# Token pairs in the first four chunks, fp32 weights on SyncE's queue and transposes by DMA in a fused linear-attention and cosine-MLP kernel

## The chip, the cores and the metric

The kernel runs on one core of a Trainium2 chip. The metric is the device time of one execution in microseconds; lower is better. Before the change it is 232.49 us, the median of three runs (231.07 to 234.35).

## The reference

Two stages follow each other. The first is a gated linear attention over 4 batches x 8 heads x 768 tokens with head size 48; the second is a two-layer network with the activation h*cos(h) on the 3072 tokens of 384 features that come out of it.

```python
f = 1.0 / (1.0 + np.exp(-f_logit))
for t in range(S):
    state = f[:, :, t, :, None] * state + np.einsum('bhd,bhe->bhde', k[:, :, t], v[:, :, t])
    y[:, :, t] = np.einsum('bhd,bhde->bhe', q[:, :, t], state)
x = y.transpose(0, 2, 1, 3).reshape(B * S, H * D)
h = x @ w_in                      # 384 -> 2048
g = h * np.cos(h)
out = g @ w_out                   # 2048 -> 384
```

All inputs and the output are fp32 in HBM; the products run in bf16 with fp32 accumulation.

## The kernel before, in words

**Chunks.** The tokens are cut into 24 chunks of 128 tokens, six to a batch. The recurrence is done chunk by chunk: within a chunk it is a masked product of queries and keys, and between chunks a state of 48 x 48 per head is carried. Chunks 0, 6, 12 and 18 start a batch and have no state to take in; chunks 5, 11, 17 and 23 end one and pass none on.

**Loads.** Each chunk needs f_logit, k, q and v, 192 KB each (L329), 128 tokens on 128 partitions and the 8 heads side by side. One token of one head is 48 fp32 numbers, so each of these transfers consists of 1024 pieces of 192 bytes. All of them stand on SyncE's queue (SP) except q and v of chunk 0, which ScalarE issues. The weights, 3 MB each for w_in and w_out, are loaded in four pieces each by GpSimd (L320), whose queue converts them to bf16 on the way. Each SP transfer waits for the transfer eight places earlier to land.

**Decay.** For a group of one or two chunks ScalarE computes exp (L345) and ln (L353) of the forget gate, TensorE sums over tokens with a triangular mask (L361, L364, called cum below), and ScalarE takes two exponentials of the sums (L371, called eb and ei). These four use one table of ScalarE functions and the cosine of the second stage another, so groups are collected (GROUPS): the exps of a collected group wait for all its f loads, and each change of table costs a load of it (L567, L496).

**Attention of a chunk n.** GpSimd, in the first chunks also VectorE, multiplies q and k with the decays (qk, L384) and casts v (vb, L388). TensorE transposes the 8 blocks of 128x128 of qk (tr, L398), ScalarE or VectorE copies them from PSUM to SBUF (qkt, L402). TensorE makes the scores (sc, L414), VectorE masks them (am, L417). TensorE makes the state's increment (ps, L428), VectorE adds it (st, L437), GpSimd scales it (sz, L443). TensorE makes the output (y, L453 and L457), a copy casts it (yb), TensorE transposes its 3 blocks (trx, L470) and a copy brings them into xT (xe, both copies L402).

**The network.** It runs over units of tokens: unit 0 is chunk 0, unit 1 chunk 1, and units 2 to 12 are two chunks each. A unit of 256 tokens has eight pieces h (L489, 6 matmuls each; two pieces fill one of two PSUM places of two banks), four cosines (L496), four products g (L499), and for each of its two chunks four pieces o (L509, 4 matmuls each), a copy ot (L512) and a store (L516). Units 0 and 1 have four pieces h of 12 narrower matmuls, two cosines and four pieces o. Piece h number j reads the w_in piece j (units 0 and 1) or j // 2 (the others); piece o number s of a chunk reads w_out piece s.

**Order.** A planner in the program (Plan.run) places all operations on the engines by their costs and priorities, and the kernel records them in that order; on the chip each engine works through its own list and waits by semaphores. Priorities before are a chunk's or unit's number plus a constant (LEAD_H, LEAD_O).

Of the kernel before, what the change touches and what calls it, by code (L numbers as in the profile page):

```python
# [15 lines left out]
class Slots:  # L16


    def __init__(self, aps, name):
        self.aps, self.name = aps, name  # L20
        self.free_at = [0.0] * len(aps)
        self.held = [False] * len(aps)

# [17 lines left out]
class Banks:  # L41
# [20 lines left out]
    def used(self, s, t):  # L62
        for i in range(s, s + self.size):
            self.base["free"][i] = max(self.base["free"][i], t)

# [35 lines left out]
class Op:  # L101
    __slots__ = ("seq", "eng", "fn", "prio", "table", "deps", "vals", "alloc", "start", "end",
                 "lat", "waiting", "after", "grp", "dma", "name", "late")


class Plan:
# [37 lines left out]
    def run(self):  # L144
        free = dict.fromkeys(("PE", "ACT", "DVE", "POOL", "SP"), 0.0)
        table, lock, bus = None, None, {}
# [9 lines left out]
        while len(order) < n:  # L156
            cand = []
            for o in ready:
                at, pe = o.late, "PE" in o.eng
# [39 lines left out]
            for v in o.alloc:  # L199
                if v.slot is None:  # L200
                    v.slot = v.pool.best()[1]
                    v.pool.take(v.slot)
            o.start = s
            free[e] = s + cost
            if o.dma is not None:
                kb, rate = o.dma
                ring = "POOL" if e == "POOL" else "SP"
                bus[ring] = max(s + cost, bus.get(ring, 0.0)) + kb * 1e3 / rate
                o.end = bus[ring] + 1700.0
# [21 lines left out]
GROUPS = [(1, 1), (2,), (2, 2), (2, 2), (2, 2), (2, 2), (2, 2)]  # L231
UNITS = [128, 128] + [256] * 11
LEAD_H, LEAD_O = 2.31, 9.45
ANCHOR = [None, None, 2, 10, 18, 26, 34]


def build(nc, cpool, ppool, q, k, v, f_logit, moe_w_in, moe_w_out, out):
# [29 lines left out]
    def zpad(t):  # L267
# [10 lines left out]
    vbS = slots("vb", 4, [128, HD])  # L278
    qktS = slots("qkt", 3, [128, 2 * NP, C])
# [4 lines left out]
    x_sb = [tl([128, KM, 256], BF16, f"xT_{i}") for i in range(n_tokens // 256)]  # L284
    gS = slots("gT", 4, [128, KF, 256])
# [5 lines left out]
    base = {"held": [False] * 8, "free": [0.0] * 8,  # L291
            "tiles": [ppool.tile([128, 1024], F32, name=f"ps_{i}") for i in range(4)]}
    phS = Banks(base, 2, [0, 2], "ph")
    scS = Banks(base, 2, [4, 6], "sc")
    p1S = Banks(base, 1, [7, 6, 5, 4], "p1")
# [18 lines left out]
    def load_weights(part, i, prio, late):  # L314
        def fn(e):
# [4 lines left out]
            nc.gpsimd.dma_start(out=dst.ap, in_=src)  # L320
        dst = w_in_v[i] if part == 0 else w_out_v[i]
        P.op(f"w{part}{i}", {"POOL": 900.0}, fn, writes=[dst], prio=prio, dma=(786, 230), late=late)

    def issue(e):
        return {"SP": nc.sync, "ACT": nc.scalar, "POOL": nc.gpsimd}[e]

    def load(t, src, b, c, prio, eng, nm):
        def fn(e):
            issue(e).dma_start(out=t.ap, in_=src[b, :, c * C:(c + 1) * C, :].rearrange("h p d -> p h d"))  # L329
        P.op(nm, {eng: 480.0}, fn, writes=[t], prio=prio, dma=(196, 240))  # L330

    xT = [Val(ap=x_sb[n // 2][:, :, n % 2 * C:n % 2 * C + C] if nc is not None else None)
          for n in range(n_tokens // C)]
    state = {}

    def decay(chunks, g, prio):
# [4 lines left out]
        for i, (b, c, n, ld) in enumerate(chunks):  # L341
            load(ft.part(lambda a, i=i: a[:, i]), f_logit, b, c, n - 0.4, "SP", f"f{n}")
# [5 lines left out]
        gates.append((first, ANCHOR[g]))  # L348
# [4 lines left out]
        P.op("ln", {"ACT": act(384 * m, "S")}, lambda e: nc.scalar.activation(  # L353
# [246 lines left out]
```

## Time and profile before

| what | value |
|---|---|
| median of 3 runs | 232.49 us |
| the profiled execution's own time | 231.37 us |
| its span in the trace | 229.5 us |
| TensorE (PE) busy | 184.0 us, 80% |
| PE weight loads (PEld) busy | 136.5 us, 59% |
| VectorE (DVE) busy | 122.4 us, 53% |
| ScalarE (ACT) busy | 134.2 us, 58% |
| GpSimd (POOL) busy | 78.9 us, 34% |
| bytes moved | 27.05 MB in 107030 packets, 100352 of them under 512 bytes |

The profile lists busy times by engine, the span in 40 slices of 5.74 us with a digit for each engine's busy tenths, the DMA queues, the chain of work that ended last (each step followed back to what released it), and groups of instructions by line. A matmul's busy time includes the time it spends in the pipeline, so what a run of matmuls really costs TensorE is read from one start to the next.

### The profile page before, as it was taken

What the parts mean: (1) busy time and instruction counts of PE and PEld (TensorE: products, weight loads), DVE (VectorE), ACT (ScalarE), POOL (GpSimd) and SP (SyncE); (2) the same over time, 40 slices, a digit from 0 to 9 for tenths busy, and PEclk for the clock granted to TensorE, in tenths of its full rate; (3) what the DMA queues carried; (4) which work ended last, traced back from release to release, by engine and by line L of the source; (5) the groups of instructions that cost most, each with busy time, mean ns of one, the idle gap of its engine ahead of it and who ended that gap; (6) DMA issues with size and microseconds to landing.
All of it is one profiled execution on the core that took longest, in us unless ns stands there. A gap on an engine that the chain in (4) does not pass through costs nothing.

```text
span 229.5 us, 4755 instructions
## 1 busy us (share of the span) xinstructions
PE 184.0 (80%) x1936; PEld 136.5 (59%) x1936; DVE 122.4 (53%) x150; ACT 134.2 (58%) x163; POOL 78.9 (34%) x121
## 2 busy tenths in 40 slices
PE   0230498455999987999979999989999899999993
PEld 0120398324777756787658776677775677776551
DVE  1150259303788629794095971568852888665000
ACT  3400667483566885758867667856688675654111
POOL 6401772029602087400763222750208611000000
PEclk9999999955799999999999999999999999999999
DMA  8999999899999398803799224781001010100211
GB/s 132 213 193 196 185 200 191 162 199 188 184 194 176 82 223 164 155 13 93 141 210 199 49 60 103 174 174 32 3 34 39 34 37 0 39 0 34 73 69 69
DMA packets 107030, 27.05 MB, mean 118 GB/s; under 512 B 100352, under 2 KB 107008, under 8 KB 107008
## 3 DMA queue, kind: packets, MB, share of 16 engines
q1 hardware_dynamic: 101216, 23.21, 53.0%
q0 software_dynamic: 3712, 3.15, 8.5%
q10 hardware_dynamic: 2080, 0.39, 1.1%
q8 instruction: 15, 0.25, 0.5%
q14 instruction: 7, 0.06, 0.1%
HBM read 25.17 MB, written 4.72 MB: 130 GB/s over the span
## 4 chain that ended last, share of the span: by engine, by line
PE 56%; DVE 11%; ACT 10%; SPq 9%; DMA 8%; issue 3%; POOL 1%; DVEq 0%; ACTq 0%; POOLq 0%
PE ps L509 25%; PE ps L489 20%; SPq L329 9%; DMA f<-in_f_logit_dram 7%; ACT qkt L402 4%; DVE gT L499 4%; PE ps L414 3%; DVE am L417 2%; PE ps L398 2%; DVE qkt L402 2%; PE ps L470 2%; DMA k<-in_k_dram 2%; ACT f L345 1%; PE ps L361 1%; DVE st L437 1%
## 5 line engine op out<-in xcount | busy, mean ns | idle before, releaser
L509 PE MATMUL ps<-w_out_bf,gT 128*128 128x384 bf16 x384 | 73.1, 330 | 6.0 <-ACT qkt L402 2.0
L489 PE MATMUL ps<-xT,w_in_bf 128*128 128x256 bf16 (+1 forms) x624 | 76.3, 270 | 1.7 <-DVE gT L499 1.7
L496 ACT ACTIVATE cosh<-ps,halfpi 128x1024 bf16<-128x1024 f32 x48 | 53.0, 1115 | 28.1 <-PE ps L489 28.0
L499 DVE TENSOR_TENSOR gT<-ps,cosh 128x1024 bf16<-128x1024 f32 x48 | 58.1, 1219 | 13.2 <-ACT cosh L496 13.0
L489 PEld LDWEIGHTS <-w_in_bf 128*128 128x128 bf16 x624 | 56.7, 101 | 11.2 <-issue 2.1
L509 PEld LDWEIGHTS <-gT 128*128 128x128 bf16 x384 | 36.1, 98 | 26.8 <-issue 8.4
L388 POOL CAST vb<-v 128x384 bf16<-128x384 f32 x24 | 12.5, 519 | 66.6 <-PE ps L457 27.8
L417 DVE TENSOR_TENSOR am<-ps,umask 128x1024 bf16<-128x1024 f32 x24 | 29.3, 1219 | 6.5 <-PE ps L414 6.4
L398 PE MATMUL ps<-ident,qk 128*128 128x128 bf16 x192 | 16.5, 234 | 14.6 <-POOL qk L384 13.2
L384 POOL TENSOR_TENSOR qk<-q,b 128x384 bf16<-128x384 f32 x21 | 21.0, 999 | 20.5 <-ACT b L371 12.9
L443 POOL TENSOR_TENSOR sz<-st,b 64x192 bf16<-64x192 f32 x32 | 16.0, 501 | 23.5 <-DVE st L437 22.2
L398 PEld LDWEIGHTS <-qk 128*128 128x128 bf16 x192 | 13.0, 103 | 17.5 <-POOL qk L384 14.4
L384 POOL TENSOR_TENSOR qk<-k,bi 128x384 bf16<-128x384 f32 x22 | 22.3, 1013 | 0.3
L345 ACT ACTIVATE f<-f 128x768 f32<-128x768 f32 (+1 forms) x13 | 9.9, 789 | 20.3 <-DMA f<-in_f_logit_dram 20.2
L402 ACT COPY qkt<-ps 128x1024 bf16<-128x1024 bf16 x13 | 13.2, 1012 | 10.3 <-PE ps L509 9.1
L361 PE MATMUL ps<-sp,umask 128*128 128x384 bf16 x24 | 8.1, 363 | 13.3 <-ACT sp L353 12.1
L402 DVE COPY qkt<-ps 128x1024 bf16<-128x1024 bf16 x11 | 7.6, 688 | 20.3 <-PE ps L509 10.6
L437 DVE TENSOR_TENSOR st<-ps,sz 128x384 f32<-128x384 f32 x16 | 8.8, 552 | 12.5 <-ACT qkt L402 11.1
L512 DVE COPY ot<-ps 128x384 f32<-128x384 f32 x12 | 6.6, 554 | 16.5 <-PE ps L509 12.0
L371 ACT ACTIVATE b<-ps 128x776 f32<-128x776 f32 (+1 forms) x13 | 10.0, 768 | 8.8 <-PE ps L364 8.5
L414 PE MATMUL ps<-qkt 48*128 48x128 bf16 x192 | 10.2, 229 | 5.6 <-DVE st L437 2.4
L364 PEld LDWEIGHTS <-sp 128*128 128x128 bf16 x96 | 5.7, 101 | 14.9 <-issue 13.5
(37 smaller groups left out, 150.8 us busy)
## 6 DMA issues: line engine op xcount, KB each, us to landing
f<-in_f_logit_dram SPq DMA_DIRECT2D x24, 192.0 KB, 4.6
k<-in_k_dram SPq DMA_DIRECT2D x24, 192.0 KB, 4.4
out_dram<-ot SPq DMA_DIRECT2D x24, 192.0 KB, 1.9
q<-in_q_dram SPq DMA_DIRECT2D x23, 192.0 KB, 4.3
v<-in_v_dram SPq DMA_DIRECT2D x23, 192.0 KB, 4.4
w_in_bf<-in_moe_w_in_dram POOLq DMA_DIRECT2D x4, 384.0 KB, 6.9
w_out_bf<-in_moe_w_out_dram POOLq DMA_DIRECT2D x4, 384.0 KB, 7.9
q<-in_q_dram ACTq DMA_DIRECT2D x1, 192.0 KB, 4.1
```

Of the source, the lines that this page charges most:

```text
L329: issue(e).dma_start(out=t.ap, in_=src[b, :, c * C:(c + 1) * C, :].rearrange("h p d -> p h d"))
L384: lambda e, j=j, src=src, dec=dec: E(e).tensor_mul(out=qk.ap[:, j, :, 0:D], in0=src.ap, in1=HB(dec.ap[:, i, 0:HD])),
L388: P.op("vb", {"POOL": 560.0}, lambda e: nc.gpsimd.tensor_copy(out=vb.ap, in_=vf.ap.rearrange("p h d -> p (h d)")), reads=[vf], writes=[vb] ...
L398: nc.tensor.transpose(out=o[:, j * NP + p, :], in_=pair(j, p), identity=ident)
L402: (nc.scalar.copy if e == "ACT" else nc.vector.tensor_copy)(out=o, in_=i_)
L414: nc.tensor.matmul(o[:, r, p, :], lhsT=qkt.ap[s, NP + p, :], rhs=qkt.ap[s, p, :], start=(p == 0), stop=(p == NP - 1))
L417: P.op("am", {"DVE": dve(1024)}, lambda e: nc.vector.tensor_mul(out=am.ap.rearrange("p r a n -> p (r a) n"), in0=sc.ap.rearrange("p (a n) ...
L443: eng().tensor_mul(out=S_out.ap[s, :, r, :], in0=srcap()[s, :, r, :], in1=bt.ap[s, i, HD:, None].broadcast_to([64, NP, D]))
L489: nc.tensor.matmul(ph.ap[:, g * T:(g + 1) * T], lhsT=w_in_bf[:, m, f0:f0 + 128], rhs=x[:, m, :], start=(g % (G // 2) == 0 and m == 0), sto ...
L496: nc.scalar.activation(out=co.ap, in_=ph.ap, func=AF.Sin, bias=halfpi),
L499: P.op("g", {"DVE": dve(1024)}, lambda e, ph=ph, co=co, gv=gv: nc.vector.tensor_mul(out=gv.ap, in0=ph.ap.rearrange("p (g t) -> p g t", t=T ...
L509: nc.tensor.matmul(po.ap[:, 0:d_model], lhsT=gT.ap[:, j, i * C:(i + 1) * C], rhs=w_out_bf[:, j, :], start=(j == 0), stop=(j == KF - 1))
```

## The change

Five things are changed together.

1. **Pairs.** In chunks 0 to 3 (NPAIR = 4) a partition holds two neighbouring tokens of four heads instead of one token of eight: partitions 0 to 63 take heads 0 to 3, partitions 64 to 127 heads 4 to 7. A piece of a transfer is then 384 bytes and there are 512 of them, in two transfers of 64 partitions each, issued one after the other. cum, tr, sc, ps and y have a form of their own for it, with new masks (incl, strict, pmask, half), a v tile with zeros (vp, filled by two casts) and more or wider matmuls: cum has 3 matmuls for 1 beside 4 narrow ones, sc 16 for 8, ps and y twice the columns. The stores of these chunks are two of 64 partitions.
2. **Weights.** They are loaded as fp32 on SP's queue into places of gT and cast to bf16 by an operation wc on GpSimd, VectorE or ScalarE. gT has 6 places for 4; xT has 5 places that are used again, for 12 that were not.
3. **Transposes by DMA.** In chunks 14 to 22 the 8 blocks of qk go from SBUF to SBUF by one DMA transpose on SP's queue (tq) instead of tr and qkt; in chunks 12 to 22 the 3 blocks of yb do (ty) instead of trx and xe.
4. **PSUM.** h has three places for two, single-bank results six banks for four, both overlapping with others.
5. **Order.** GROUPS is cut otherwise, with single chunks first; the priorities are a table (PR) with an entry for each load, decay, chunk, turn and unit, and the exps of the first collected group no longer wait for all of its f loads. The planner's costs and its model of the DMA queue are changed.

```diff
-GROUPS = [(1, 1), (2,), (2, 2), (2, 2), (2, 2), (2, 2), (2, 2)]
+GROUPS = [(1, 1, 1), (1,), (2,), (2, 2), (2, 2), (2, 2), (2, 2), (2,)]
 UNITS = [128, 128] + [256] * 11
-LEAD_H, LEAD_O = 2.31, 9.45
-ANCHOR = [None, None, 2, 10, 18, 26, 34]
+NPAIR = 4
+FREE_GROUPS = 1
+TURN_QK = range(14, 23)
+TURN_Y = range(12, 23)
+PR = {
...
-    gS = slots("gT", 4, [128, KF, 256])
+    xS = slots("xT", 5, [128, KM, 256])
+    gS = slots("gT", 6, [128, KF, 256])
...
-    phS = Banks(base, 2, [0, 2], "ph")
-    scS = Banks(base, 2, [4, 6], "sc")
-    p1S = Banks(base, 1, [7, 6, 5, 4], "p1")
+    phS = Banks(base, 2, [0, 2, 4], "ph")
+    scS = Banks(base, 2, [4, 6, 2], "sc")
+    p1S = Banks(base, 1, [7, 6, 5, 4, 3, 2], "p1")
...
-            nc.gpsimd.dma_start(out=dst.ap, in_=src)
-        P.op(f"w{part}{i}", {"POOL": 900.0}, fn, writes=[dst], prio=prio, dma=(786, 230), late=late)
+            nc.sync.dma_start(out=view(), in_=src)
+        P.op(f"w{part}{i}", {"SP": 420.0}, fn, writes=[stage], prio=prio, dma=2080.0)
+        P.op("wc", {"POOL": 2100.0, "DVE": 900.0, "ACT": act(1536, "S")}, lambda e:
+             cast(e, dst.ap, view()), reads=[stage], writes=[dst], prio=PR["wc"][4 * part + i])
...
+            for r in range(2):
+                (nc.scalar if e == "ACT" else nc.sync).dma_start(
+                    out=t.ap[64 * r:64 * r + 64].rearrange("p (h e) d -> p h (e d)", e=2),
+                    in_=tok[4 * r:4 * r + 4].rearrange("h (p e) d -> p h (e d)", e=2))
...
-        for o in firsts[g]:
-            o.deps.update(loads)
+        if g >= FREE_GROUPS:
+            for o in firsts[g]:
+                o.deps.update(loads)
...
-        P.op("tr", {"PE": mm(128, 8)}, tr, reads=[qk], writes=[pt], prio=prio)
+        if n in TURN_QK:
+            P.op("tq", {"SP": 420.0}, lambda e: nc.sync.dma_start_transpose(
+                out=qkt.ap, in_=qk.ap.rearrange("p j h d -> p (j h d)")),
+                reads=[qk], writes=[qkt], prio=PR["tq"][n], dma=2000.0)
+        else:
+            pt = Val(p1S)
+            P.op("tr", {"PE": mm(128, 8)}, tr, reads=[qk], writes=[pt], prio=prio)
...
-        px, x = Val(p1S), xT[n]
+        x = xT[n]
+        if n in TURN_Y:
+            P.op("ty", {"SP": 420.0}, lambda e: nc.sync.dma_start_transpose(out=x.ap, in_=yb.ap),
+                 reads=[yb], writes=[x], prio=PR["ty"][n], dma=1200.0)
+            return
```

The first place is the start of SP's list, before the change: f, k, q, v by 192 KB (the number behind a name is the buffer).

```order
L329 DMA f_73<-in_f_logit_dram 128x8x48
L329 DMA k_76<-in_k_dram 128x8x48
L329 DMA f_74<-in_f_logit_dram 128x8x48
L329 DMA k_77<-in_k_dram 128x8x48
L329 DMA q_81<-in_q_dram 128x8x48
L329 DMA v_85<-in_v_dram 128x8x48
L329 DMA f_75<-in_f_logit_dram 128x8x48
L329 DMA k_78<-in_k_dram 128x8x48
```

The same place with the change: L383 are weight pieces into gT, L399 halves of a paired load (x2 is one load), L396 loads of a chunk from 4 on.

```order
L383 DMA gT_160<-in_moe_w_in_dram 128x3x512
L399 DMA f_94<-in_f_logit_dram 64x4x96 x2
L399 DMA v_105<-in_v_dram 64x4x96 x2
L399 DMA v_106<-in_v_dram 64x4x96 x2
L399 DMA f_95<-in_f_logit_dram 64x4x96 x2
L399 DMA f_96<-in_f_logit_dram 64x4x96 x2
L399 DMA k_97<-in_k_dram 64x4x96 x2
L399 DMA k_98<-in_k_dram 64x4x96 x2
L399 DMA q_102<-in_q_dram 64x4x96 x2
L383 DMA gT_161<-in_moe_w_in_dram 128x3x512
L399 DMA v_107<-in_v_dram 64x4x96 x2
L396 DMA k_99<-in_k_dram 128x8x48
```

A weight piece now stands first, the three f of chunks 0 to 2 come before k and q, and a chunk from 4 on already has its k in row 12. Up to and with the last w_in piece, row 24, SP's list has 4 weight pieces, 15 paired loads (q of chunk 0, the sixteenth, is on ScalarE) and 5 whole loads; from row 25 to k of chunk 6, row 39, it has 12 whole loads and the 4 w_out pieces.

The second place is PE's list around the scores of chunk 14, before: tr (L398) of chunk 14, a piece h around the transposes of an output (L470), and sc (L414); one row stands for each group of equal rows and their weight loads.

```order
L398 MATMUL ps_155<-ident,qk_102 128x128
...
L489 MATMUL ps_153<-xT_133,w_in_bf 128x256
...
L470 MATMUL ps_156<-ident,yb_127 128x128
...
L489 MATMUL ps_153<-xT_133,w_in_bf 128x256
...
L414 MATMUL ps_155<-qkt_114 128x128
```

The same place with the change, from ps (L575) of chunk 14 to its scores (L550): L671 are matmuls of o, 8 and 4 of them, L651 of h, 12 and 12, and the second L575 is ps of chunk 15.

```order
L575 MATMUL ps_178<-vb_131,qk_125 128x96
...
L671 MATMUL ps_178<-w_out_bf,gT_161 128x384
...
L651 MATMUL ps_177<-xT_157,w_in_bf 128x256
...
L651 MATMUL ps_175<-xT_157,w_in_bf 128x256
...
L575 MATMUL ps_178<-vb_130,qk_124 128x96
...
L671 MATMUL ps_178<-w_out_bf,gT_161 128x384
...
L550 MATMUL ps_176<-qkt_141 128x128
```

The transposes are gone from this place, and between ps, which needs the same qk as the turn, and the scores, which need the turned one, there is now work of the network.

The third place is SP's list in the second half, with the change: turns of qk (L517) and of yb (L622) among stores (L685) and loads; before, no transposes stood on this list.

```order
L517 DMA_TRANSPOSE qkt_139<-qk_123 128x8x128
L396 DMA k_97<-in_k_dram 128x8x48
L396 DMA q_102<-in_q_dram 128x8x48
L685 DMA out_dram<-ot_169 128x384
L622 DMA_TRANSPOSE xT_158<-yb_154 128x3x128
L517 DMA_TRANSPOSE qkt_141<-qk_125 128x8x128
L396 DMA k_98<-in_k_dram 128x8x48
```

Nine L517 and eleven L622 stand on this list from its row 84 on. A load behind a turn is issued only when the turn's qk or yb has been written.

## Rows read from the trace of the kernel before

**Rows 1.** The page's slices of 5.74 us: busy tenths of PE and DMA

```profile
PE   0230498455999987999979999989999899999993
DMA  8999999899999398803799224781001010100211
```

**Rows 2.** Busy us and count by engine, granted clock, DMA share, GB/s, by stretch

```profile
0.00:30.10 30.10, 7.29 (x83) 5.54 (x84) 6.59 (x13) 8.69 (x15) 12.64 (x29) 1.00 1.17 185
30.10:42.00 11.90, 11.16 (x175) 10.19 (x172) 10.26 (x14) 7.62 (x8) 4.63 (x7) 1.00 1.20 193
42.00:57.00 15.00, 6.79 (x59) 4.21 (x59) 2.63 (x5) 8.75 (x10) 6.97 (x11) 0.66 1.15 182
57.00:71.00 14.00, 13.59 (x144) 10.43 (x142) 10.95 (x13) 7.90 (x10) 4.67 (x6) 0.87 1.13 193
71.00:226.20 155.20, 145.22 (x1485) 106.14 (x1483) 91.95 (x108) 100.78 (x120) 50.00 (x70) 1.00 0.40 87
...
200.00:226.20 26.20, 24.39 (x165) 15.79 (x162) 7.35 (x6) 8.63 (x12) 0.00 (x0) 1.00 0.12 46
```

**Rows 3.** Chain that ended last, up to 58 us: start, length, what

```profile
19.26 4.40 DMA f<-in_f_logit_dram
...
35.50 7.80 DMA f<-in_f_logit_dram
...
47.73 4.07 DMA k<-in_k_dram
...
51.82 1.96 POOL qk L384 x2
```

**Rows 4.** Timeline of SP's queue: start, us of the issue

```profile
0.74 0.43 SPq L329 DMA_DIRECT2D f<-in_f_logit_dram  x1
...
48.74 0.89 SPq L329 DMA_DIRECT2D q<-in_q_dram  x1
49.72 1.01 SPq L329 DMA_DIRECT2D k<-in_k_dram  x1
```

**Rows 5.** DMA queues: packets, MB, share of 16 engines; issues: KB, us to landing

```profile
q0 software_dynamic: 3712, 3.15, 8.5%
q10 hardware_dynamic: 2080, 0.39, 1.1%
...
k<-in_k_dram SPq DMA_DIRECT2D x24, 192.0 KB, 4.4
out_dram<-ot SPq DMA_DIRECT2D x24, 192.0 KB, 1.9
```

**Rows 6.** Timeline of PE, 63 to 73 us: start, busy, matmuls

```profile
63.96 0.61 PE L398 MATMUL ps<-ident,qk 128*128 128x128 bf16 x8
64.40 0.82 PE L489 MATMUL ps<-xT,w_in_bf 128*128 128x256 bf16 x6
...
68.03 0.40 PE L414 MATMUL ps<-qkt 48*128 48x128 bf16 x8
68.36 0.83 PE L489 MATMUL ps<-xT,w_in_bf 128*128 128x256 bf16 x6
69.02 0.33 PE L428 MATMUL ps<-vb,qk 128*128 128x96 bf16 x4
69.19 0.81 PE L509 MATMUL ps<-w_out_bf,gT 128*128 128x384 bf16 x4
69.84 1.47 PE L489 MATMUL ps<-xT,w_in_bf 128*128 128x256 bf16 x12
...
72.66 0.33 PE L470 MATMUL ps<-ident,yb 128*128 128x128 bf16 x3
72.83 0.38 PE L489 MATMUL ps<-xT,w_in_bf 128*128 128x256 bf16 x2
```

**Rows 7.** Groups by line: count, busy us, mean ns of one, idle before

```profile
L567 ACT ACT_TABLE_LOAD x6 | 7.7, 1283 | 2.1 <-issue 2.0
...
L402 DVE COPY qkt<-ps 128x1024 bf16<-128x1024 bf16 x11 | 7.6, 688 | 20.3 <-PE ps L509 10.6 <-PE ps L398 9.3 <-PE ps L428 0.4
```

More of the change, by code (lines that the diff above doesn't have):

```diff
@@ L22, in __init__ @@
         self.held = [False] * len(aps)
+        self.last, self.now = [[] for _ in aps], [[] for _ in aps]
     def best(self):
@@ L60, in take, with users, used @@
             self.base["held"][i] = True
-    def used(self, s, t):
+            self.base["last"][i], self.base["now"][i] = self.base["now"][i], []
+    def users(self, s):
+        return sum((self.base["last"][i] for i in range(s, s + self.size)), [])
+    def used(self, s, t, o):
         for i in range(s, s + self.size):
             self.base["free"][i] = max(self.base["free"][i], t)
+            self.base["now"][i].append(o)
     def drop(self, s):
@@ L102 @@
     __slots__ = ("seq", "eng", "fn", "prio", "table", "deps", "vals", "alloc", "start", "end",
-                 "lat", "waiting", "after", "grp", "dma", "name", "late")
+                 "lat", "waiting", "after", "grp", "dma", "name", "prior", "cost")
 class Plan:
@@ L205, in run @@
             if o.dma is not None:
[L206 to L209, printed above, removed]
+                bus = max(s + cost + 700.0, bus) + o.dma
+                o.end = bus + 1250.0
             else:
@@ new lines, in ln @@
+        def ln(e):
+            o, i_ = sp.ap[:, 0:m, :, 0:D], ft.ap[:, 0:m]
+            if chunks[0][2] < NPAIR:
+                o = sp.ap.rearrange("p m h d -> p (m h) d").rearrange(
+                    "p (e h) d -> p h e d", e=2)[:, 0:4 * m, :, 0:D]
+                i_ = i_.rearrange("p m h d -> p (m h) d").rearrange("p (h e) d -> p h e d", e=2)
+            nc.scalar.activation(out=o, in_=i_, func=AF.Ln, bias=1.0)
+        P.op("ln", {"ACT": act(384 * m, "S")}, ln, reads=[ft], writes=[sp], prio=prio, table="E", grp=g)
@@ L426, in pes @@
             def pes(e):
+                if pm:
+                    o = ps.ap[:, 0:HD].rearrange("p (g a n) -> p g a n", g=2, a=2)
+                    for p in range(2):
+                        for x in range(2):
+                            nc.tensor.matmul(o[:, :, p, :], lhsT=twin(1, p, x),
+                                             rhs=vtwin()[:, :, x, 2 * p:2 * p + 2, :],
+                                             start=(p == 0 and x == 0), stop=(p == 1 and x == 1))
+                    return
                 for p in range(NP):
@@ L474, in attend @@
              reads=[px], writes=[x], prio=prio)
+    UNIT = {sum(UNITS[:i]): i for i in range(len(UNITS))}
     def moe(t0, T):
         n0, n1 = t0 // C, (t0 + T) // C
-        xs, gT = xT[n0:n1], Val(gS)
+        xs, gT, xw = xT[n0:n1], Val(gS), starts[t0]
         G = 1024 // T
@@ L539, in build @@
                 t0 += units.pop(0)
-    for o, at in gates:
-        if at is not None:
-            o.deps.add(cosines[at - 1])
+    for o, g in gates:
+        if PR["gate"][g] is not None:
+            o.deps.add(cosines[PR["gate"][g] - 1])
+    P.gates, P.cosines = gates, cosines
     return P
```

210 lines of the change are left out of this document (160 added, 50 removed), and 12 rows, old and new, of the table PR.

## The prediction

> **What bounds the kernel now.** I read the slices first. The DMA engines are full for 13 of 40 slices, some 75 us; TensorE is idle in most of the first ten and near full from about 57 us on [rows 1]. The windows put numbers on that: up to 57 us TensorE is busy for 7.3, 11.2 and 6.8 us of 30.1, 11.9 and 15.0, while 182 to 193 GB/s flow at a DMA share above 1; from 71 to 226.2 us it is busy for 145.2 of 155.2 us at full clock, with a DMA share of 0.40 [rows 2]. So there are two stages: first loads set the pace, then TensorE. The chain of the first stage says which loads: f of chunks 2 and 3 until 23.7 us, f of the four chunks 4 to 7 until 43.3, because the exps of a collected group wait for all of them, and only then k of chunk 4, which lands at 51.8 and is multiplied on GpSimd until 53.8 [rows 3]. ScalarE (100.8 us) and VectorE (92.0) do not bind in the second stage [rows 2].
>
> **The first stage: prices.** While the queue is full, SP issues a 192 KB load per 1.0 us [rows 4]; that is its price. A bf16 weight piece takes 8.5% of 16 engines over 229.5 us, divided by 8: 2.44 us [rows 5]. As fp32 it writes twice the bytes: upper bound 4.9, if written bytes count. The lower bound comes from the stores, which also move fp32 rows of 1536 bytes: in the last window they run at 46 GB/s with a share of 0.12 [rows 2], 383 GB/s on full engines, and a piece of 786 KB takes 2.05 us. I take that, the nearest in shape. A paired load has half the pieces: 0.5 us if only their number counts, 1.0 if only bytes do. A 192-byte piece costs 19.4 ns (1.1% x 16 x 229.5 us / 2080 [rows 5]), a 1536-byte one 64 (1536 bytes at 383 / 16 GB/s); on that line 384 bytes cost 25.8 ns, and a load 25.8 / 38.8 of 1.0 us, 0.67. But it is issued twice, and an issue takes 0.43 us at least [rows 4], so 0.9 for SP unless it is ahead, which it is only behind weight pieces. I take 0.8.
>
> The Trainium skill speaks against such halves: by DMA: Bandwidth & Descriptors, Rules for kernel authors, two transfers to disjoint partition halves serialize on the same 16 engines, and one of 128 partitions is advised. By that rule alone a paired load is 1.0 us as before, and the gates below come 3.2 us later; the trace shows no half transfer.
>
> **The first stage: gates.** The second half of unit 0 needs the last w_in piece, row 24 of SP's list. Up to it stand 4 weight pieces, 16 paired loads and 5 whole ones: 8.2 + 12.8 + 5.0 = 26.0 us; with the start at 0.7 us [rows 4] and 1.9 us for an undisturbed landing, the store's [rows 5], it is there at 28.6. VectorE casts it in about 1.0 us (1.5 times a 1024-column copy of 0.69 [rows 7]), which nothing hides. What now stalls last, chunk 4's k, is row 12 and lands by 18 us. The next gate is k of chunk 6, row 39: 12 whole loads and 4 pieces more, 20.2 us, landed at 48.8; after the two qk products, 1.96 us [rows 3], tr of chunk 6 can start at 51. TensorE's own list gives nearly the same: between the two gates stand 12 pieces h and 10 o at 0.66 and 0.65 us, 14.4 us, and some 5 us of attention and sums, 19.4 in all, which from 29.6 end at 49.0 if nothing waits. Since cosines, exps and three table loads stand between on ScalarE, I allow 2 us and take **53**. Then attention of chunks 0 to 5 with the decay sums of 6 to 9, all h of units 0 to 2, and 10 pieces o are done.
>
> Before, the last h of unit 2 ends at 69.0 us, with 5 pieces o done (the next starts at 69.19) [rows 6]. The 5 missing ones cost 0.65 each (69.19 to 69.84), 3.25 us; against them stand two tr (0.44), one sc (0.33) and one ps (0.17) that it has and the changed one has not, 1.4 us. So it reaches the same work at about 71 us, and the change gains **18 us** here. The extra matmuls of the pair forms lie in this stage beside loads and cost nothing; were TensorE the bound there, eight sc matmuls more a chunk would cost at most one sc more, 0.33 us, four times. The granted clock of 0.66 between 42 and 57 us [rows 2] mixes the levels 1.2 and 2.4 GHz and follows TensorE's idleness there; I count nothing for its going.
>
> **The second stage.** Nine tr of 0.44 us and eleven trx of 0.17 us (72.66 to 72.83) [rows 6] leave TensorE: 4.0 + 1.9 = **5.9 us**. Their copies, and the weight casts that come instead, are on engines with room; two table loads more, 1.28 us each [rows 7], lie on ScalarE, which is idle for a third of this stage.
>
> The turns put waits in their place. No row shows a turn. A qk turn moves 256 KB from SBUF to SBUF; bounds for its landing are 1.9 us, a lone store of 192 KB, and 15 us, eight blocks each priced as such a lone transfer. The nearest row with neighbours on the queue is a load, 4.4 us [rows 5], and I take that: the queue is half empty here. Against it stands what TensorE has to do between. From ps to sc of chunk 14 these are two o, four h, a ps and one o: 1.3 + 2.6 + 0.17 + 0.65 = 4.7 us. Chunks 15 and 16 have 7 and 6 us, chunks 18 to 21 over 8; chunk 22 has more than its list shows, since qk is ready well before ps. From y to the h that reads its turned chunk the least is about 5 us, in units 10 to 12, from which yb's cast (half a us) comes off. So 4.4 us fits narrowly and I price the waits at nothing; a turn of 7 us would cost some 8 us at those four places. Behind a late turn on SP stand loads that are wanted two chunks later, and stores.
>
> The 10 us of TensorE idleness in this stage I leave: a third h place closes some, new order may open others. The tail after 226.2 us stays.
>
> **Sum.** 229.5 - 18 - 5.9 = 205.6 us span; the profiled execution took 231.37, 1.9 more than its span, so 207.5. The median of the runs shown is 1.1 us above that execution, inside their spread. I forecast **208 us**.
>
> **Rivals.**
> - *Dearer loads.* A weight piece writes 848 bytes a packet in 84 ns (8.5% / 3712) and a load 192 in 19.4 [rows 5], both 0.10 ns a byte. If written bytes count, even midway, an fp32 piece costs 3.5 us and a paired load with its two issues 1.05; the gate of chunk 6 comes 8 x 1.45 + 16 x 0.25 = 15.6 us later at most, and it ends at 216 to 223, about 220. Against it: the stores' rate. Chance 0.17.
> - *Closer packing.* No 2 us of waits before chunk 6, paired loads at 0.67 (2 us), and half of the 10 idle us closed by the third h place: 199. For it: an h place is free again only after 1.1 us of cosine and 1.2 of product. Chance 0.15.
> - *Turns bind the queue, slower than before.* If a turn handles its blocks one after another and turns do not overlap, nine of T and eleven of 3/8 T make 13.1 T of SP's queue, between the first ty, where TensorE is at about 90 us (53 plus some 34 us of listed work at nine tenths), and the scores of chunk 22, some 30 us of h and o before the last piece, at 172. These 82 us are filled at T = 6.3; the old time is reached at 13.1 T = 82 + 24, T = 8.1, or 1.0 us a block. Bytes at the load's rate make a block 0.17 us, a lone transfer 1.9; between them, at T = 10, it ends at 208 + 49 = 257. Chance 0.09: the upper half of what the rows allow, but overlap of turns would undo it. VectorE: DVE Perf Modes, The three transpose paths, in the Trainium skill, gives 1309 ns for a 128x128 bf16 block by DMA against 390 on TensorE and advises TensorE where PSUM will do; by that, eight in a row, T = 10.5 and an estimated 264 us. No run here shows it yet.
> - *No change:* the gain at the start given back by waits at turns of 7 to 8 us and by loads behind them, 226 to 234. Chance 0.05.
>
> **How the numbers follow.** The forecast, 203 to 214, has 0.54; with closer packing and most of dearer loads the range 198 to 221 holds a little over 0.8. Faster by over 2%, about what a measurement of this kernel can tell from no change, means under 227.8: 0.54 + 0.15 + 0.16, 0.85. Within 2%: 0.06. Slower: 0.09.
>
> **What would show it.** Right: TensorE's list reaches tr of chunk 6 at 50 to 55 us; SP spaces halves at 0.4 to 0.5 us and weight pieces at some 2; the stretch behind it is 5.9 us of matmuls lighter; turns land in 3 to 5 us and PE's waits on them sum to under 3 us. Wrong: weight pieces near 4 us, a late f of chunks 6 to 9, PE waiting long for scores of chunks 14 to 22 or for h of units 7 to 12, SP's queue standing at turns while loads behind it are awaited.

## The result, and the profile after

The changed kernel takes 215.03 us, the median of four runs (213.22 to 216.39), against 231.86 for the kernel before on the same chip: a ratio of 0.925, 95% interval 0.914 to 0.936. Timed again later it took 214.59 us (212.79 to 214.86, six runs), ratio 0.927 [0.923, 0.930]. So it is 17 us faster, where 24 were forecast. Every ratio is to the kernel before timed beside that run and compares fast executions alone, so a median of all executions (230.88 us with the turns alone) need not match its ratio exactly. The profiled execution took 213.22 us and spans 211.4; a trace taken when it was timed again spans 212.8.

Busy time by engine, slices of 5.28 us, and issues with their median us to landing, of the changed kernel:

```profile
PE 174.7 (83%) x1871; PEld 130.2 (62%) x1871; DVE 137.8 (65%) x179; ACT 130.5 (62%) x157; POOL 68.7 (32%) x108
...
PE   0152685678989888999989899999998999989983
...
DMA  6969799999998988979988999845955241011113
...
gT<-in_moe_w_in_dram SPq DMA_DIRECT2D x4, 768.0 KB, 5.5
...
xT<-yb SPq DMA_TRANSPOSE x11, 2.9
...
qkt<-qk SPq DMA_TRANSPOSE x9, 3.6
```

TensorE is 9.3 us less busy than before. The DMA row is new in the first slices: 6, 9, 6, 9, 7, where before it stood at 8 and 9 from the first slice on [rows 1]: the engines are *less* full at the start than they were. The turns land in 3.6 us (qk) and 2.9 us (yb).

Busy us and count by engine, granted clock, DMA share and GB/s by stretch, as in [rows 2]; 63.0 us is where TensorE reaches tr of chunk 6:

```profile
0.00:30.00 30.00, 11.71 (x138) 9.56 (x139) 15.70 (x34) 12.81 (x23) 7.80 (x27) 0.89 0.88 200
30.00:42.00 12.00, 7.34 (x145) 6.42 (x143) 9.19 (x12) 10.48 (x12) 7.54 (x11) 1.00 0.94 241
42.00:52.00 10.00, 7.79 (x94) 6.51 (x92) 9.88 (x12) 6.80 (x7) 1.99 (x4) 1.00 1.04 235
52.00:63.00 11.00, 10.14 (x110) 6.85 (x108) 7.45 (x10) 10.21 (x13) 3.76 (x4) 1.00 0.96 240
63.00:211.40 148.40, 137.72 (x1397) 100.90 (x1394) 95.61 (x114) 90.16 (x105) 47.57 (x64) 1.00 0.64 133
```

Before, the second stage ran from 71 to 229.5 us, 158.5 us with 145.2 busy [rows 2]; now it takes 148.4 with 137.7 busy. Of these 10.1 us, 7.5 are busy time gone and 2.6 idle time less. The first stage gave 8 us (71 to 63; in the second trace tr of chunk 6 starts at 64.3), where 18 were forecast. The two gates of the prediction, VectorE's cast of the last w_in piece and what TensorE does behind it:

```profile
37.32 1.75 DVE L389 CAST w_in_bf<-gT 128x1536 bf16<-128x1536 f32 x1 [0.75 <-DMA gT<-in_moe_w_in_dram]
```

```profile
39.13 1.51 PE L651 MATMUL ps<-xT,w_in_bf 128*128 128x128 bf16 x24 [1.46 <-DVE w_in_bf L389]
...
63.03 0.61 PE L515 MATMUL ps<-ident,qk 128*128 128x128 bf16 x8
```

The second half of unit 0 starts at 39.1 us (forecast 29.6), tr of chunk 6 at 63.0 (forecast 53). Between the two lie 23.9 us, forecast 23.4. Of the delay of 10 us 9.5 are there by the first gate: 8.7 until the cast starts (forecast 28.6), which the loads ahead of it made, and 0.75 by a longer cast. SP's issues there, start and length, "x4" being two paired loads:

```profile
6.62 2.59 SPq L399 DMA_DIRECT2D f<-in_f_logit_dram  x4
9.25 2.59 SPq L399 DMA_DIRECT2D k<-in_k_dram  x4
11.89 1.27 SPq L399 DMA_DIRECT2D q<-in_q_dram  x2
...
16.86 3.33 SPq L399 DMA_DIRECT2D f<-in_f_logit_dram  x2
...
28.14 2.36 SPq L399 DMA_DIRECT2D v<-in_v_dram  x2
...
31.20 0.70 SPq L383 DMA_DIRECT2D gT<-in_moe_w_in_dram  x1
```

A half takes SP 0.65 us from one issue to the next, a paired load 1.3, one behind the other without a pause. The prediction had 0.8. Of the thirty halves ahead of the last w_in piece three stood longer, 1.3 to 2.7 us, as the one at 16.86 and the one at 28.14; in those stretches the DMA engines are full:

```profile
15.00:20.00 5.00, 2.35 (x34) 1.78 (x32) 1.92 (x3) 2.79 (x4) 0.26 (x1) 1.00 1.10 263
...
25.00:30.00 5.00, 4.13 (x53) 3.72 (x54) 3.06 (x4) 3.06 (x6) 0.00 (x0) 0.79 1.16 287
```

The last w_in piece is issued at 31.2 us and has landed when the cast starts, 6.1 us later.

### The profile page after: what moved, and what is told of

Read it like the earlier page. It is cut to its first block, busy times and chain, and to the rows that moved or that the text cites. A ratio compares the mean times of both kernels' runs of the same rounds, so it can differ in the third digit from the quotient of the medians.

```text
span 211.4 us, 4701 instructions
## 1 busy us (share of the span) xinstructions
PE 174.7 (83%) x1871; PEld 130.2 (62%) x1871; DVE 137.8 (65%) x179; ACT 130.5 (62%) x157; POOL 68.7 (32%) x108
## 4 chain that ended last, share of the span: by engine, by line
PE 50%; DVE 7%; ACT 1%; issue 1%; DVEq 0%; ACTq 0%
PE ps L671 23%; PE ps L651 20%; DVE gT L661 3%; PE ps L612 1%; PE ps L550 1%; ACT ot L674 1%; DVE am L554 1%; DVE st L584 1%; PE ps L458 1%; PE ps L600 1%; PE ps L575 1%; DVE yb L525 1%; DVE qkt L525 1%; PE ps L515 1%; PE ps L630 1%
## 5 line engine op out<-in xcount | busy, mean ns | idle before, releaser
L671 PE MATMUL ps<-w_out_bf,gT 128*128 128x384 bf16 x384 | 70.1, 326 | 6.8 <-DVE st L584 2.1
L651 PE MATMUL ps<-xT,w_in_bf 128*128 128x256 bf16 (+1 forms) x624 | 69.8, 264 | 4.1 <-DVE w_in_bf L389 2.3
L651 PEld LDWEIGHTS <-w_in_bf 128*128 128x128 bf16 x624 | 55.9, 98 | 12.4 <-DVE w_in_bf L389 2.5
L671 PEld LDWEIGHTS <-gT 128*128 128x128 bf16 x384 | 35.6, 97 | 29.0 <-issue 8.5
L590 POOL TENSOR_TENSOR sz<-st,b 64x192 bf16<-64x192 f32 x32 | 16.1, 503 | 33.1 <-DVE st L584 30.0
L554 DVE TENSOR_TENSOR am<-ps,umask 128x1024 bf16<-128x1024 f32 x20 | 24.4, 1218 | 2.9 <-ACT bi L468 1.3
L674 ACT COPY ot<-ps 128x384 f32<-128x384 f32 x16 | 7.7, 478 | 21.8 <-PE ps L671 16.7
L422 ACT ACTIVATE f<-f 128x768 f32<-128x768 f32 (+1 forms) x14 | 10.1, 747 | 9.7 <-DMA f<-in_f_logit_dram 9.6
L468 ACT ACTIVATE b<-ps 128x776 f32<-128x776 f32 (+1 forms) x14 | 10.2, 729 | 8.8 <-issue 4.6
L389 DVE CAST w_in_bf<-gT 128x1536 bf16<-128x1536 f32 x4 | 7.0, 1752 | 9.2 <-DMA gT<-in_moe_w_in_dram 9.2
L525 DVE CAST yb<-ps 128x384 bf16<-128x384 f32 x14 | 7.8, 554 | 6.6 <-PE ps L671 2.1
L389 POOL CAST vb<-v 128x384 bf16<-128x384 f32 x9 | 4.5, 503 | 20.3 <-PE ps L612 16.5
L448 PE MATMUL ps<-sp,incl 128*128 128x384 bf16 x4 | 2.0, 501 | 10.7 <-ACT sp L437 10.7
L468 ACT ACTIVATE bi<-ps 128x768 f32<-128x768 f32 (+1 forms) x14 | 10.1, 723 | 0.7 <-PE ps L511 0.7
L437 ACT ACTIVATE sp<-f 128x768 bf16<-128x768 f32 (+1 forms) x14 | 10.0, 744 | 0.1
L389 DVE CAST vb<-v 128x384 bf16<-128x384 f32 x11 | 5.9, 535 | 5.3 <-PE ps L612 5.2
```

Source lines behind the costliest of these rows:

```text
L389: (nc.scalar.copy if e == "ACT" else nc.vector.tensor_copy if e == "DVE" else nc.gpsimd.tensor_copy)(out=o, in_=i_)
L422: first = P.op("exp", {"ACT": act(384 * m, "S")}, lambda e: nc.scalar.activation(out=fl(ft.ap), in_=fl(ft.ap), func=AF.Exp, scale=-1.0), r ...
L468: nc.scalar.activation(out=out_.ap[:, 0:m, :], in_=i, func=AF.Exp, scale=s)
L525: (nc.scalar.copy if e == "ACT" else nc.vector.tensor_copy)(out=o, in_=i_)
L554: P.op("am", {"DVE": dve(1024)}, lambda e: nc.vector.tensor_mul(out=am.ap.rearrange("p r a n -> p (r a n)").rearrange("p (a n) -> p a n", ...
L590: eng().tensor_mul(out=S_out.ap[s, :, r, :], in0=srcap()[s, :, r, :], in1=bt.ap[s, i, HD:, None].broadcast_to([64, NP, D]))
```

## Experiments

The first question is the start: does SP's issuing hold it, or the DMA engines, or the weights? The second is the later stage: what are turns, places and order worth there? "The changed kernel" is at 214.6 to 215.0 us throughout.

**No pairs.** The list of operations and their order stay; only what chunks 0 to 3 emit is plain.

```diff
+EMIT = 0
-            if n >= NPAIR:
+            if n >= EMIT:
                 nc.sync.dma_start(out=t.ap, in_=tok.rearrange("h p d -> p h d"))
```

> Chunks 0 to 3 are loaded, computed and stored in the plain form, one transfer of 128 partitions for each load; the order of the work on each engine stays. Theory A (the start is held by SyncE, which needs about 0.65 us for each half of a paired load, 1.3 us for both): fifteen loads cost 1.0 us in place of 1.3, so the cast of the last w_in piece starts 3 to 5 us before the 37.3 us that it has with pairs, and the kernel ends at 211 to 213. Rival B (half the pieces are what pays, as my prediction priced it, 0.8 us a paired load against 1.0): the cast starts 3 us later and it ends at 217 to 219.

Measured: 211.34 us (210.64 to 212.19), ratio to before 0.909 [0.904, 0.915]: 3.3 to 3.7 us faster than the changed kernel, and the fastest version here. VectorE's cast of the last piece, and the stretch up to it:

```profile
35.38 1.75 DVE L390 CAST w_in_bf<-gT 128x1536 bf16<-128x1536 f32 x1 [1.47 <-DMA gT<-in_moe_w_in_dram]
```

```profile
10.00:35.40 25.40, 14.66 (x190) 12.11 (x190) 15.63 (x23) 16.63 (x27) 5.53 (x10) 0.98 0.95 223
```

The end came as theory A had it, the gate only in part: 1.9 us earlier, not 3 to 5, and tr of chunk 6 at 61.7. Against the second trace of the changed kernel (cast at 37.9, tr of chunk 6 at 64.3, end at 212.8) all three come 2.4 to 2.6 us earlier, so the gain is made by the first gate. Now the engines are near full, at a share of 0.95. So the pairs, meant to shorten the loads, lengthen the kernel; but behind SP's issues the engines stand as the next bound.

**Halves on two queues.** The second half of eight early paired loads goes to ScalarE's queue.

```diff
-                (nc.scalar if e == "ACT" else nc.sync).dma_start(
+                (nc.scalar if e == "ACT" or r and nm + str(n) in SPLIT else nc.sync).dma_start(
+SPLIT = ("f0", "v1", "v0", "f1", "f2", "k0", "k1", "q1")
```

> The second halves of eight of the first paired loads (f of chunks 0 to 2, v of 0 and 1, k of 0 and 1, q of chunk 1) are issued by ScalarE ahead of its first table load; all else stays. Theory A (SyncE's issue binds): SyncE is rid of 8 x 0.65 = 5.2 us, part of it refilled by its waits; the cast of the last w_in piece starts 3 to 5 us before 37.3 and the kernel ends at 211 to 213; ScalarE's first exp starts about 1 us later than its 7.6. Rival B (the DMA engines bind the start, whoever issues): the cast stays at 36.5 to 37.5 and the end at 214 to 216.

Measured: 213.89 us, ratio 0.920 [0.915, 0.926], about 1 us faster, which the intervals cannot tell from no change. The same stretch of the changed kernel and of this one:

```profile
8.70:15.70 7.00, 3.75 (x29) 2.98 (x29) 2.43 (x7) 3.92 (x9) 0.91 (x2) 1.00 0.68 158
```

```profile
8.70:15.70 7.00, 1.77 (x14) 1.24 (x13) 1.49 (x5) 4.26 (x8) 0.90 (x2) 1.00 1.01 232
10.00:36.00 26.00, 17.09 (x229) 14.32 (x229) 16.63 (x24) 18.69 (x30) 4.99 (x9) 1.00 0.99 222
```

In the changed kernel the DMA engines work at 0.68 of their time there, 158 GB/s: SP's issuing binds, as theory A says. With the second queue they are full, and now they bind: 222 GB/s up to 36 us, as without pairs (223). The cast starts at 35.8, between what the two theories said, and so does the end lie. Both causes are real, one behind the other. Over these stretches, which hold whole loads and weight pieces too, halves on full engines carry no more bytes a second than whole loads do. That is what the Trainium skill says in DMA: Bandwidth & Descriptors, Rules for kernel authors: two transfers to disjoint partition halves serialize, from one queue or two. The traces agree (222 against 223 GB/s), and SP's second issue comes on top.

**Prices by themselves.** Ahead of the kernel, transfers alone, in a single execution.

> Ahead of the unchanged kernel SyncE's queue alone moves, back to back: 16 whole loads of 192 KB; 16 paired loads as two halves each on SyncE; 16 paired loads with the second half on ScalarE's queue; 6 fp32 weight pieces; 6 turns of qk's shape and 5 of yb's (sources zeroed; nothing of it is used by the kernel behind it, whose time is longer by it). It prices what the first stage waits for. Theory A (issue binds, the engines could do more): whole loads 1.0 to 1.3 us each, paired ones 1.3 us each on SyncE with the DMA engines at 0.6 to 0.8 of their time, and 0.8 to 1.0 us with both queues; weight pieces about 2.0 us. Rival B (two halves of 64 partitions cost the engines as much as a whole load or more): paired loads at a DMA share near 1.0 on SyncE already, and no cheaper with both queues. Turns: as the kernel's run shows SyncE busy 1.2 to 1.3 us for each, about 1.3 us apart.

Measured, by stretch (the columns of the windows above): whole loads; the first paired loads on SP; paired loads on both queues; weight pieces; turns of 8 blocks; turns of 3.

```profile
3.00:14.00 11.00, 0.00 (x0) 0.00 (x0) 6.13 (x9) 0.00 (x0) 5.49 (x9) 1.00 1.09 215
14.50:18.50 4.00, 0.00 (x0) 0.00 (x0) 0.00 (x0) 0.00 (x0) 0.00 (x0) 1.00 0.93 197
20.00:40.00 20.00, 0.00 (x0) 0.00 (x0) 0.00 (x0) 0.00 (x0) 0.00 (x0) 1.00 0.76 180
...
54.00:62.00 8.00, 0.00 (x0) 0.00 (x0) 0.00 (x0) 0.00 (x0) 0.00 (x0) 1.00 1.00 354
...
69.00:73.10 4.10, 0.00 (x0) 0.00 (x0) 0.00 (x0) 0.00 (x0) 0.00 (x0) 1.00 0.95 179
73.10:79.50 6.40, 0.00 (x0) 0.00 (x0) 0.00 (x0) 0.00 (x0) 0.00 (x0) 1.00 0.49 99
```

And SP's issue of a whole load and of a half, ns min/median/max:

```profile
L719 SPq DMA_DIRECT2D k<-in_k_dram x4: 451/682/1028, 0.7 to 2.7; - x4
```

```profile
L723 SPq DMA_DIRECT2D k<-in_k_dram x12: 596/616/759, 14.4 to 42.7; - x12
```

A whole load of 196.6 KB costs 0.91 us (215 GB/s), a weight piece of 786 KB 2.2 us (354 GB/s). A paired load costs SP 2 x 0.616, 1.23 us, plus small gaps; with both queues 1.09 us (180 GB/s) while the engines are 0.76 busy, 0.83 us of their time. The 4 us from 14.5 on still hold the last whole loads, and ScalarE's halves joined at 18.5 us, earlier than meant, so paired loads on SP alone have no clean row of DMA share. Per byte the engines save some 9 to 17% by the larger pieces, not the third that the prediction's line through two points gave; in the stretches of the experiments above, with other loads among them, none of it shows.

**Weights on GpSimd's queue.**

```diff
-            nc.sync.dma_start(out=view(), in_=src)
+            nc.gpsimd.dma_start(out=dst.ap, in_=src)
...
-             cast(e, dst.ap, view()), reads=[stage], writes=[dst], prio=PR["wc"][4 * part + i])
+             None, reads=[stage], writes=[dst], prio=PR["wc"][4 * part + i])
```

> The eight weight pieces are loaded by GpSimd's queue, which turns them to bf16 on the way, at the places in the order where SyncE loaded them; the casts on VectorE and ScalarE fall away; all else stays. Theory A: SyncE loses 4 issues of 0.6 us ahead of the last w_in piece and the cast of 1.75 us behind it falls away, so the second half of unit 0's h starts 3 to 4 us before the 39.1 us that it has, end at 211 to 213. Rival C (bytes and packets of the pieces pay: 2.44 us a piece through GpSimd's queue by the trace of the kernel before, about 2 us as fp32): 8 x 0.4 = 3 us later in all, end at 217 to 219, with SyncE's loads slowed.

Measured: 219.84 us, ratio 0.947 [0.942, 0.952], 5 us slower. GpSimd's issues of the last w_out pieces, then TensorE's waits ahead of the second half of unit 0, and tr of chunk 6:

```profile
25.75 1.55 POOL L383 DMA_DIRECT2D w_out_bf<-in_moe_w_out_dram  x2
...
31.58 0.81 POOL L383 DMA_DIRECT2D w_out_bf<-in_moe_w_out_dram  x1
```

```profile
37.95 0.62 PE L511 MATMUL ps<-ident,qk 128*128 128x128 bf16 x8 [4.26 <-POOL qk L482]
...
41.99 0.82 PE L570 MATMUL ps<-vp,qk 128*128 128x192 bf16 x4 [3.26 <-ACT vp L389]
...
45.87 2.72 PE L651 MATMUL ps<-xT,w_in_bf 128*128 128x128 bf16 x24
```

```profile
70.23 0.61 PE L515 MATMUL ps<-ident,qk 128*128 128x128 bf16 x8
```

The second half of unit 0 starts 6.7 us later, and no longer because of w_in: TensorE waits 7.5 us for qk and vp of chunk 3, whose q and v land late. GpSimd's list has nothing that holds the pieces back, so all four w_out pieces are issued by 32.4 us, among the loads of chunk 3; on SP's queue the first of them went out at 33.7 us, behind those loads. So theory A is wrong, and rival C has about the time (217 to 219) but not the cause: the trace shows the place of the weights among the loads, not the price of a piece. That reading was not tried by itself.

**No turns.** The twenty transposes return to TensorE at the turns' places, VectorE copies them out, and a fixed order keeps every other instruction.

```diff
-            P.op("tq", {"SP": 420.0}, lambda e: nc.sync.dma_start_transpose(
-                out=qkt.ap, in_=qk.ap.rearrange("p j h d -> p (j h d)")),
+        pt = Val(p1S)
+        P.op("tq" if n in TURN_QK else "tr", {"PE": mm(128, 8)}, tr, ...
```

> All twenty turns by DMA are undone: TensorE transposes qk of chunks 14 to 22 and yb of 12 to 22 where the DMA turns stood in the order, VectorE copies the results; every other instruction keeps its place and engine. Theory (as in the prediction: the turns are worth TensorE's nine times 0.44 and eleven times 0.17 us, and nothing waits for them): 5.9 us more, end at 219 to 223, with TensorE's busy time up by about 6 us. Rival D (VectorE's copies and a sixth PSUM place being taken stall TensorE too): 8 us or more, end above 223. Rival E (the turns are worth nothing, since TensorE had idle time there and waited for turns instead): within 2 us of 215.

Measured: 228.84 us, ratio 0.986 [0.981, 0.992]: 14 us slower, not 6. The second stage, to be set beside the last row of the changed kernel's windows:

```profile
63.70:226.80 163.10, 146.07 (x1502) 106.97 (x1499) 104.37 (x134) 90.26 (x105) 47.47 (x64) 1.00 0.44 99
```

TensorE is 8.4 us busier and idle for 17.0 us in place of 10.7, 6.3 more. Its waits there are many and short; those on VectorE's copies sum to 2.4 us for qkt and 2.2 for xT, where the changed kernel has none and 0.4. Rival D holds: a transpose on TensorE costs its matmuls and, in an order made without it, a round trip through PSUM.

**Turns issued twice, and turns issued late.** First each turn twice into its tile; then a turn into a spare tile ahead of each, whose edit this is.

```diff
-            P.op("tq", {"SP": 420.0}, lambda e: nc.sync.dma_start_transpose(
-                out=qkt.ap, in_=qk.ap.rearrange("p j h d -> p (j h d)")),
+            P.op("tq", {"SP": 420.0}, lambda e: [nc.sync.dma_start_transpose(
+                out=o, in_=qk.ap.rearrange("p j h d -> p (j h d)")) for o in (spare[n % 3], qkt.ap)],
```

> Each of the twenty turns by DMA is issued twice, one behind the other, so that what reads it waits for the second. Theory (the order leaves slack, as the prediction took 4.7 us against a landing that turned out at 3.6 and 2.9): a turn lands some 1.3 to 2 us later, at about 5 us, and the end moves by 0 to 3 us, 215 to 218. Rival (turns sit on the path or bind SyncE's queue): 20 x 1.25 = 25 us more of SyncE's time between 105 and 186 us show in loads, stores and scores, and the end is 223 or more.

> Ahead of each of the twenty turns by DMA a turn of the same source into a spare tile is issued, which nothing reads and nothing waits for: each real turn is issued 1.25 us later and lands so much later, without SyncE standing for a landing as it did with the turns into one tile twice. Theory (slack of about 5 us against landings of 3.6 and 2.9 us, now 4.9 and 4.2): TensorE waits 2 to 6 us in all for turns, end at 216 to 221. Rival (there is no slack left behind the turns and SyncE's queue is near its bound, as the run with turns twice showed +36): half of that or more, end at 230 and later.

Measured: 251.54 us with turns twice, 224.51 (ratio 0.971 [0.965, 0.977]) with late ones. Waits with turns twice (total, times, longest), of TensorE, then of SP:

```profile
PE ps L550 <- DMA qkt<-qk: 18.1, 7, 5.4
...
PE ps L651 <- DMA xT<-yb: 7.3, 5, 3.3
```

```profile
SPq L517 <- DMA qkt<-qk: 18.7, 9, 3.6
...
SPq L622 <- DMA xT<-yb: 14.6, 11, 2.1
```

The second turn into the same tile waits on SP until the first has landed, which the expectation overlooked: SP stood for 33 us, and with the forty issues the turns held it for 87. From the first issue to the second landing a pair of qk took 6.2 to 8.2 us, one of yb 4.6 to 5.8. TensorE's busy time with turns twice:

```profile
PE 190.8 (76%) x1871; PEld 138.9 (55%) x1871; DVE 137.2 (54%) x179; ACT 130.6 (52%) x157; POOL 68.4 (27%) x108
```

Of the 40.5 us by which this trace is longer (251.9 against 211.4), 24.4 are idle time; 16.1 are the same 1871 matmuls taking longer, at a mean granted clock of 0.925 in place of 0.984. This went the rival's way. TensorE's waits with late turns are fewer:

```profile
PE ps L551 <- DMA qkt<-qk: 5.3, 2, 2.7
...
PE ps L653 <- DMA xT<-yb: 1.6, 2, 1.1
```

This run ended between its theory (216 to 221) and its rival (230 and later), 9.5 to 9.9 us behind the changed kernel. But its turns are later by more than the 1.25 us that was meant: the delays add up on SP's list, whose issues follow each other almost without a gap from 125 to 151 us. The turn of chunk 17 and the scores that read it, in the changed kernel and with late turns:

```profile
130.57 1.24 SPq L517 DMA_TRANSPOSE qkt<-qk  x1
...
139.84 0.40 PE L550 MATMUL ps<-qkt 48*128 48x128 bf16 x8
```

```profile
138.31 2.37 SPq L518 DMA_TRANSPOSE spare<-qk  x1
140.77 1.26 SPq L518 DMA_TRANSPOSE qkt<-qk  x1
...
144.00 0.40 PE L551 MATMUL ps<-qkt 48*128 48x128 bf16 x8 [2.64 <-DMA qkt<-qk]
```

Up to these scores TensorE runs 1.5 us behind the first trace of the changed kernel; its second trace runs 1.3 behind, so this is not the turns' doing. The turn is issued 10.2 us later, 8.7 more than TensorE is late. In the changed kernel it lies ready some 5.7 us before it is read (landing in 3.6), and what is left over, with a landing in 3.2 there, is the wait of 2.6. So the slack is real: by the trace of the changed kernel the nine turns of qk lie ready 2.6 to 7.7 us before their scores. What has little to spare is SP's queue. Against the second trace (212.8 us) the late turns cost 9.3 us: 6.9 of waits, and some 1.6 at a granted clock of 0.83 from 140 to 150 us, a mix of the levels 1.2 and 2.4 GHz behind the first long wait, where the changed kernel has 1.00; 0.8 stay open.

**Turns alone, PSUM places alone.** Both in the kernel before, whose planner places the work again: first the twenty turns, then the three lines of places (ph, sc, p1).

> The turns alone: the kernel before with the twenty transposes done by DMA as in the changed kernel (priority that of the transposes they replace), all else of before, its planner placing the work. Theory (turns take 5.9 to 7.4 us of matmuls off TensorE wherever there is slack): 224 to 227. Rival (the gain hangs on an order made for it: between ps and sc the order before leaves less than the 3.6 us of a landing): TensorE waits for scores of chunks 14 to 22, end at 231 to 245.

> The PSUM places alone: the kernel before with three places for h, three for sc and six single ones that overlap, its planner placing the work again. Theory (a third place for h closes idle time of TensorE): 226 to 230. Rival (places that overlap help only with an order made for them, since one h takes two single places; the run with the old places in the new order was 32 us slower): 235 and later.

Measured: 230.88 us, ratio 0.989 [0.984, 0.994], with the turns; 280.14 us, ratio 1.211, with the places. The first kernel's busy times:

```profile
PE 178.7 (78%) x1831; PEld 132.0 (58%) x1831; DVE 118.5 (52%) x142; ACT 126.7 (55%) x151; POOL 78.9 (35%) x121
```

TensorE has 5.3 us less to do, as forecast (5.9), and the kernel gains half of it, 2.6 us by the ratio (1.4 to 3.8 by its interval); its waits for turns sum to only 1.6 us, so the rest went into other idle time. The places alone do great harm, 49 us by the spans (278.1 against 229.5). 16.5 of these are the same 1936 matmuls at a mean granted clock of 0.883 in place of 0.970; the rest is idle time. The longest wait, for qk of GpSimd, is 20.5 us, but it was 13.2 before and so explains 7 of them. Which of the overlapping places causes the loss was not followed up.

**Old places in the new order, and the order alone.**

```diff
-    phS = Banks(base, 2, [0, 2, 4], "ph")
+    phS = Banks(base, 2, [0, 2], "ph")
```

> The PSUM places are those of before (two for h, two for sc, four single ones), with the order of the changed kernel kept wherever a place is to be had. Theory (the third place closes some of TensorE's idle time, as the prediction's closer packing had it): 3 to 8 us slower, end at 218 to 223, with waits of h and o for places. Rival (the third place does nothing, since ScalarE's cosine and VectorE's product come in time): within 2 us of 215.

> Pairs, weights on SyncE, turns and PSUM places are all undone; only the order, the groups and gates of the changed kernel stay, kept wherever a place is to be had. If the single effects add up (no pairs -4, weights +5, turns +14, PSUM +3 to 8, on 215), it ends at 233 to 238, no faster than the kernel before: the order by itself is worth nothing. Rival (the order, with f of the first chunks early and smaller groups, is what made the start shorter): 222 to 228, with the h pieces of unit 0 ending well before the 45 us or so at which the kernel before has them.

Measured: 247.35 us with the old places (ratio 1.068), 264.78 us with everything undone but the order (1.139). With the old places TensorE's longest wait is for an h place:

```profile
PE ps L651 <- DVE gT L661: 16.1, 14, 2.5
```

In the changed kernel that wait is 0.8 us in all, so it makes 15 of the some 24 us of idle time that this trace has more. The single effects on the changed kernel add up to about 262 us (215 - 4 + 5 + 14 + 32), near the 264.8 measured, but the order without the parts is 33 us *slower* than the order before. So the order brings nothing by itself: it is made for these places and turns. Neither of the two expectations on x6 was near.

**The changed kernel again,** beside the last three.

> The changed kernel unaltered, timed again beside the others: 213 to 216.5, as before, to set against the version without pairs, 211.3.

Measured: 214.59 us, ratio 0.927 [0.923, 0.930]; the version without pairs (0.909 [0.904, 0.915]) lies outside that interval. Its gates, to set beside those of the first trace and of the version without pairs:

```profile
37.87 1.75 DVE L389 CAST w_in_bf<-gT 128x1536 bf16<-128x1536 f32 x1 [0.51 <-DMA gT<-in_moe_w_in_dram]
```

```profile
64.33 0.61 PE L515 MATMUL ps<-ident,qk 128*128 128x128 bf16 x8
```

## Why the prediction was right, and where not

**The two stages** were right: loads set the pace to 63 us, then TensorE.

**Price of a paired load: the step that failed.** 0.8 us was taken between 0.67 for the engines and 0.9 for SP. The 0.9 came from two of the shortest issue of a whole load, 0.43 us [rows 4]. A half takes 0.61 to 0.65, so SP needs 1.3. The thirty halves on SP's list took it 22.5 us, where the sum had 12.8 (with ScalarE's load), and so the last w_in piece was issued at 31.2 us in place of 24.7. Behind it stands a second error: the engines' 0.67 is 0.83 by the run of prices, so even with SP relieved the cast came at 35.8. The rule that the prediction weighed and set aside (the Trainium skill, DMA: Bandwidth & Descriptors, Rules for kernel authors) was the better guide: by it the prediction made a paired load 1.0 us.

**Landing of the last piece: too short.** The sum gave it 2.05 us on the engines and the landing of a lone store, 1.9. It took 6.1 us from its issue, 2.1 more, behind loads that were still under way (DMA share 0.94 from 30 to 42 us). With the 6.5 us of late issue this makes the 8.7 by which the cast started late (37.3 against 28.6).

**Weight piece, whole load:** 2.05 and 1.0 us forecast, 2.2 and 0.91 measured. Right; the rival of dearer pieces (3.5 us) is refuted although its time, 220, was not far off. Undoing this part cost 5 us; the trace points to w_out, which then overtakes loads that are wanted sooner.

**Cast:** 1.75 us where 1.0 was taken from a bf16 copy [rows 7]. A cast from fp32 is another operation; 0.75 us.

**From gate to gate:** 23.9 against 23.4 us. Right, and in its parts too: TensorE is busy for 20.2 us (19.4 of listed work) and waits 3.7 (4 allowed). So the miss at the first gate went through unabridged.

**Second stage:** 10.1 us gained against 5.9. TensorE's busy time accounts for 7.5; about half a microsecond of that is the comparison point, since the count of equal work at 71 us left out the decay sums of chunks 8 and 9, which the kernel before still had to make. Busy time also counts more for a transpose than the prediction's start to start (0.33 against 0.17 us for a trx [rows 6]), so the two do not compare exactly. 2.6 us are idle time, which the prediction left unchanged on purpose. By the runs the worth of turns depends on the order: 2.6 us in the old one, 14 in the new. How much the third h place gives by itself stays open, since each order fails with the other's places.

**Waits for turns at nothing:** right. The landing was put at 4.4 us and is 3.6 and 2.9; the changed kernel shows no wait for a turn. The slack was called narrow; for qk the trace has 2.6 us at the least. That a turn of 7 us would cost 8 us was not tested: turns twice, at about that, cost 36, but there SP stood too, and the clock fell. This is the rival of turns that bind the queue: 87 us of SP's time in turns against the 82 that it counted, with loads and stores on the same list. Its premise for the changed kernel itself, blocks one after another, for which it named 1309 ns each (the Trainium skill, VectorE: DVE Perf Modes, The three transpose paths), does not hold here: eight blocks land in 3.1 to 5.7 us, and 1.2 to 1.3 us is what a whole turn takes SP where it does not stand.

**Sum:** the span was forecast at 205.6 and is 211.4: 10.0 late at the start, 4.2 early behind it. The measured 215 us lies one above the forecast's 203 to 214 and inside the wider 198 to 221. That it is there is in part luck: the two errors have opposite signs, and without the 4.2 us, which nothing in the prediction foresaw, it would be 219. Of the signs that were named, tr of chunk 6 at 50 to 55 us and halves at 0.4 to 0.5 us did not come; the weight pieces, the lighter second stage and the landings did.

## What to carry to other kernels

Price a transfer twice, once by the engines that move it and once by the queue that issues it, with the issue time of its own shape; cutting one transfer in two to make its pieces longer can double the second price, as here (1.2 to 1.3 us for 0.45 to 0.6), and the gain in the first was small. An order worked out for a set of buffers and a set of operations is one thing with them: here undoing the places cost 32 us and undoing the turns 14, while in the old order the turns brought 2.6 and the places cost 49. Where a wait is hidden by slack, read from the trace how long each result lies ready before it is used; a test that adds work to the same queue measures the queue's slack with it.

## What was unexpected of the hardware

- SP needs longer to issue a half load of 64 partitions (596 ns at least) than a whole one with four times its pieces (451 ns at least).
- A DMA transpose holds SP for 1.2 to 1.3 us, of 8 blocks as of 3. Back to back they follow each other at about that distance, the ones of 8 blocks at a DMA share of 0.95, those of 3 at 0.49. The landing differs by little: 3.3 us against 2.3.
